# A fused SSM and token-mixing block: the short convolution of k for the fourth and fifth chunk, summed in place and moved out of step two

## The chip, the core and the metric

The kernel runs on one core of one Trainium2 chip. The metric is the device time of one execution in microseconds (us); the kernel's time is the median of its runs. TensorE (PE) multiplies matrices into PSUM, VectorE (DVE), ScalarE (ACT) and GpSimd (POOL) work on PSUM and SBUF (POOL on SBUF only, here), and SyncE (SP) issues the DMAs. Each engine takes its instructions in the order in which the program wrote them; they wait for one another by semaphores.

## The reference

```python
def _A_ref(q, k, v, shift_k, ssm_k, ssm_D):
    # short causal depthwise convolution of k (4 taps)
    k_pad = jnp.pad(k, ((0, 0), (ks - 1, 0), (0, 0)))
    for t in range(ks):
        k_shift = k_shift + k_pad[:, t:t + S, :] * shift_k[:, ks - 1 - t][None, None, :]
    kv = k_shift * v
    # long causal convolution of kv with ssm_k per channel, by FFT of length 2 S
    y = ... + kv * ssm_D
    return q * y

h = _layernorm(x) * (1 + ca) + sa
x = x + ga * _A_ref(h, A_k, A_v, A_shift_k, A_ssm_k, A_ssm_D)
h = _layernorm(x) * (1 + cb) + sb
x = x + gb * _B_ref(h, B_w1, B_b1, B_w2, B_b2)      # the token-mixing MLP with gelu
```

S = 2048 positions, D = 640 channels, F = 1728; sa to gb come from silu(c) @ w_mod. The change concerns `k_shift` and `kv` alone.

## The kernel before

The first part of the kernel, about 295 of its 669 us, does the long convolution in five chunks c = 0 to 4 of 128 channels (`NC = 5`). Each chunk's transform has stages on PE, and what the other engines do stands between them in the program's order, which is written out by hand (`manual_schedule`):

- *Step one* (`step1(side, t)`, line 230), four calls for the data (side 0, from tile `x`, which holds kv) and four for the kernel ssm_k (side 1, from `p`); ACT copies each result into `z`.
- *Step two* (`f2(g)`, line 249), eight groups g. PE multiplies `z` by constants into PSUM, ACT copies half of it into `kt`, then DVE forms two products per group (`p<-pst,kt`, called one group later) and POOL adds them into `y` (`y<-p`).
- *The inverses*: `i2(0)`, `i2(1)` (line 280) from `y` into `z`, then `i1(0)`, `i1(1)` (line 300). Among them stand step one of the next chunk: side 0, t = 0 and 1 ahead of `i2(0)`, t = 2 behind `i2(0)`, t = 3 behind `i2(1)`; side 1, t = 0 between `i1(0)` and `i1(1)`, t = 1 to 3 behind both. DVE scales q's part (`po`, `aux<-aux,g`) and multiplies the results by it, in `gate(c, ps, half)` (`aux<-pst,aux`); POOL adds that to x, SP writes x back (`spill`).

PSUM results of these stages take three buffers in turn (`psum()`, `ring = [0, 1, 2]`): the fourth result needs the buffer of the first.

The short convolution is DVE's side work. Tile `in` holds k's rows (`KX`: 3 rows of halo and 32 rows of 64 channels) and v's (`VX`). A chunk is done in four groups of eight rows. For a group, `kv_ops(g)` gives eight instructions of 128 x 512: one product into a sum in PSUM (`tap`), three pairs of a product into `kt` and an addition to the sum, and the product of the sum with v into `x`. After a group's product, `kv_loads` issues the loads of k and v for the next chunk into the rows that came free. `kv` strings the four groups together, and the list `fill` keeps what is not yet issued; `dv(n)` issues the next n of it at hand-chosen places. In an iteration c the convolution that is issued belongs to chunk c + 2.

For c = 1 and 2 (chunks 3 and 4), `dv(7)` stands ahead of `i2(0)`, `dv(3)` behind step one's t = 3, `dv(3)` between `i1(1)` and the second gate, `dv(11)` after the last step one: 24 of the 32 instructions. The eight that are left are issued in step two of iteration c + 1, between the products of its groups. The convolution of chunk 2 is put in `fill` in iteration 0 and runs mostly in step two of c = 1.

`load_ks(c + 2)` loads ssm_k for a later chunk; POOL adds ssm_D to it (`perm_add`) in step two of the next iteration.

Of the kernel before, what the change touches and what calls it, by code (L numbers as in the profile page):

```python
# [16 lines left out]
NC = D // DC  # L17
# [33 lines left out]
def mixer_kernel(ctx: ExitStack, tc: tile.TileContext, q, k, v, shift_k, ssm_k, ssm_D, w1, b1, w2, b2, c,  # L51
# [90 lines left out]
    def load_k(c, g, engs=(sync, sync)):  # L142
        for h in range(2):
            r = slice(64 * h, 64 * h + 64)
            engs[h].dma_start(KX[r, 3 + 8 * g:11 + 8 * g],
                           dram(k, 8 * g * D + DC * c + 64 * h, [[32 * D, 64], [D, 8], [1, 64]]))
# [7 lines left out]
    def load_halo(c):  # L154
        for h in range(2):
            sync.dma_start(KX[64 * h + 1:64 * h + 64, 0:3],
                           dram(k, 29 * D + DC * c + 64 * h, [[32 * D, 63], [D, 3], [1, 64]]))
# [27 lines left out]
    def kv_ops(g, eng=dve):  # L185
        S_, T_, W_ = (SV, TV, TAP) if eng is dve else (PS_.rearrange("p (n i) -> p n i", i=64),
                                                       PT.rearrange("p (n i) -> p n i", i=64), PW)
        w = lambda s: W_[:, None, s, :].to_broadcast([128, 8, 64])
        kx = lambda s: KX[:, 8 * g + 3 - s:8 * g + 11 - s, :]
        ops = [lambda: TT(eng, S_, kx(3), w(3), ALU.mult)]  # L190
        for s in (2, 1, 0):
            ops.append(lambda s=s: TT(eng, T_, kx(s), w(s), ALU.mult))
            ops.append(lambda: TT(eng, S_, S_, T_, ALU.add))
        ops.append(lambda: TT(eng, X.rearrange("p (n i) -> p n i", i=64)[:, 8 * g:8 * g + 8], S_,
                              VX[:, 8 * g:8 * g + 8], ALU.mult))
        return ops
# [11 lines left out]
    def kv(c_next, gs=((0,), (1,), (2,), (3,))):  # L208

        ops = []  # L210
        for gl in gs:
            o = kv_ops(gl[0])

            def end(gl=gl, last=o.pop()):
                last()
                if c_next is not None:
                    for g in gl:
                        kv_loads(c_next, g)
            ops += o + [end]
        return ops  # L220


    def step1(side, t, later=False):

# [313 lines left out]
    def dv(n):  # L538
        for _ in range(min(n, len(fill))):
            fill.pop(0)()  # L540

    x1s = lambda c, j: lambda: dve.bn_stats(bst[:, j, c, :], XR(j, DC * c, DC))
    for c in range(NC):
# [104 lines left out]
        elif cn is not None:  # L648
            for t in range(2):
                step1(0, t)  # L650
            perm(cn)
            if c + 2 < NC:
                fill.extend(kv(c + 3 if c + 3 < NC else None))
            else:
                fill.extend(x1s(cc, j) for cc in range(c) for j in range(16))
        else:
            t = mem("w1", 4096, "wb1")
            blk[1] = j16(t[:, 0:2048]), j16(t[:, 2048:4096])
            mod_load(3, 3, T_z[:, 0:1920])
            mod_load(3, 4, T_z[:, 1920:3840])  # L660
            sync.dma_start(P, wc[:, 2048:4096])
            for kk in range(3):
                mod_part(tap, kk, pl[kk])
            t = mem("in", 4288, "wb3")
            blk[3] = j16(t[:, 0:2048]), j16(t[:, 2048:4096])
            run(po)
            split_third(0, False, True)
            for f in (1, 3):
                split_third(f)
                split_rows(0, X, (f,))  # L670
                split_rows(1, T_aux[:, 0:2048], (f,))
            split_rows(0, X, (0,), False, True)
            split_rows(1, T_aux[:, 0:2048], (0,), False, True)
        if c:
            if cn is not None:
                dv(7)
            i2(0)
            if cn is None:
                split_rows(3, P, (1, 3))
                split_rows(3, P, (0,), True, False)  # L680
                mod_part(tap, 3, pl[3])
                i2(1, dve)
                mod_part(tap, 4, pl[4])
                t = mem("y", 4096, "wb2")
                blk[2] = j16(t[:, 0:2048]), j16(t[:, 2048:4096])
                break
            run(po)
            step1(0, 2)
            i2(1)
            step1(0, 3)  # L690
            dv(3 if cn < NC - 1 else 28)
        if c and c + 2 < NC:
            load_ks(c + 2)
        if cn == NC - 1:
# [7 lines left out]
        for half in range(2):  # L702
            ps = i1(half)
            if c and half:
                dv(3)
            elif c:
                k0 = step1(1, 0, True)
            gate(c, ps, half, pool if c else None)
# [412 lines left out]
    def product(n):  # L1121
        w_ = of(n)[1]
        bank[n] = psum()[:, 0:320]
        wh, wl = W.pop(n)
        for m, i in enumerate(SETS + ((6, 5) if n < 4 else (5, 6))):
            rh, rl = moving[w_](i)
            for k, (w, r) in enumerate(((wh, rh), (wh, rl), (wl, rh))):
                pe.matmul(bank[n], w[:, i].bitcast(F32R), r.bitcast(F32R), start=m == 0 and k == 0,  # L1128
                          stop=m == 6 and k == 2)
# [97 lines left out]
```

## Time and profile before

| | |
|---|---|
| median of 3 runs | 666.49 us (665.19 to 666.98) |
| profiled execution, its own time | 671.21 us |
| its span, first to last instruction | 669.4 us |
| PE busy | 619.5 us (93%) |
| DVE busy | 501.9 us (75%) |
| ACT busy | 309.7 us (46%) |
| POOL busy | 108.1 us (16%) |
| mean granted clock of PE | 0.982 |

Rows of the timeline give start, busy time, engine, line, operation, output<-input, and in brackets the idle time of the engine before it with what ended it. `SPq` is the time in which SP's queue issued a DMA. Rows of the table by windows give a stretch, its length, busy time of PE, PE's weight loads, DVE, ACT and POOL (with counts), the clock granted to PE, the share of the DMA engines' time and GB/s. Rows of the groups give how many instructions of a kind there are, their busy time and the mean of one in ns. Times are in us from the span's start.

### The profile page before, as it was taken

What the parts mean: (1) busy time and instruction counts of PE and PEld (TensorE: products, weight loads), DVE (VectorE), ACT (ScalarE), POOL (GpSimd) and SP (SyncE); (2) the same over time, 40 slices, a digit from 0 to 9 for tenths busy, and PEclk for the clock granted to TensorE, in tenths of its full rate; (3) what the DMA queues carried; (4) which work ended last, traced back from release to release, by engine and by line L of the source; (5) the groups of instructions that cost most, each with busy time, mean ns of one, the idle gap of its engine ahead of it and who ended that gap; (6) DMA issues with size and microseconds to landing.
All of it is one profiled execution on the core that took longest, in us unless ns stands there. A gap on an engine that the chain in (4) does not pass through costs nothing.

```text
span 669.4 us, 20749 instructions
## 1 busy us (share of the span) xinstructions
PE 619.5 (93%) x9073; PEld 597.8 (89%) x9073; DVE 501.9 (75%) x860; ACT 309.7 (46%) x483; POOL 108.1 (16%) x120
## 2 busy tenths in 40 slices
PE   0599878899998999999999999999999999999997
PEld 0598568788997989689999999999999999999997
DVE  6688569969969948789974213846689889888886
ACT  0574475545735647667765224334243332333331
POOL 5284027413324127000000000000000000000000
PEclk9999789999999999879999999999999999999999
DMA  9968988727438525414006630885598565345601
GB/s 179 213 194 225 391 172 159 168 54 165 83 70 221 180 51 156 172 33 95 0 1 126 119 71 1 189 234 144 174 365 268 173 179 154 102 144 169 188 31 41
DMA packets 175472, 98.01 MB, mean 146 GB/s; under 512 B 89843, under 2 KB 165398, under 8 KB 175126
## 3 DMA queue, kind: packets, MB, share of 16 engines
q1 hardware_dynamic: 170834, 95.38, 54.0%
q10 hardware_dynamic: 4548, 1.31, 1.1%
q8 instruction: 71, 1.16, 0.7%
q14 instruction: 19, 0.16, 0.1%
HBM read 79.63 MB, written 19.14 MB: 148 GB/s over the span
## 4 chain that ended last, share of the span: by engine, by line
PE 71%; DVE 16%; DMA 6%; issue 3%; SPq 2%; ACT 1%; POOL 0%; ACTq 0%; DVEq 0%; POOLq 0%
PE pst L1128 26%; PE pst L463 19%; PE pst L230 9%; PE pst L249 7%; PE pst L280 5%; PE pst L993 4%; DVE tap L60 3%; DVE kt L60 2%; DMA aux<-in_A_ssm_k_dram 2%; PE pst L300 2%; DMA aux<-in_w_mod_dram 2%; DVE p L60 1%; SPq L532 1%; PE tap L364 1%; DMA in<-in_A_k_dram 1%
## 5 line engine op out<-in xcount | busy, mean ns | idle before, releaser
L249 PE MATMUL pst<-z,w 128*64 128x64 f32 x2560 | 78.9, 223 | 11.0 <-DVE p L60 6.0
L249 PEld LDWEIGHTS pst<-z,w 128*64 128x64 f32 x2560 | 76.8, 138 | 13.7 <-issue 10.4
L230 PE MATMUL pst<-v,x 128*64 128x128 f32 x640 | 45.7, 302 | 24.2 <-DVE x L60 23.7
L230 PEld LDWEIGHTS pst<-v,x 128*64 128x64 f32 x640 | 43.6, 221 | 24.9 <-POOL t L488 23.7
L235 ACT ACTIVATE z<-pst 128x1024 f32<-128x1024 f32 (+2 forms) x45 | 41.4, 931 | 43.6 <-PE pst L230 24.9
L60 POOL TENSOR_TENSOR y<-p 128x256 f32<-128x256 f32 x72 | 54.1, 776 | 40.1 <-DVE p L60 39.7
L60 DVE TENSOR_TENSOR p<-pst,kt 128x512 f32<-128x512 f32 x80 | 50.8, 681 | 10.5 <-ACT kt L255 9.6
L280 PEld LDWEIGHTS pst<-v,y 32*128 32x128 f32 x1280 | 39.4, 193 | 4.2 <-issue 2.7
L280 PE MATMUL pst<-v,y 32*128 32x64 f32 x1280 | 41.2, 279 | 1.6 <-issue 1.0
L255 ACT ACTIVATE kt<-pst 128x512 f32<-128x512 f32 x40 | 23.9, 598 | 36.7 <-PE pst L249 20.9
L230 PE MATMUL pst<-v,p 128*64 128x128 f32 x640 | 37.3, 274 | 1.4 <-ACT p L177 1.2
L230 PEld LDWEIGHTS pst<-v,p 128*64 128x64 f32 x640 | 35.3, 137 | 2.2 <-ACT p L177 1.4
L1128 PE MATMUL pst<-r_z,m_w 128*128 128x320 f32 x198 | 37.2, 309 | 0.0
L60 DVE TENSOR_TENSOR tap<-tap,kt 128x512 f32<-128x512 f32 x51 | 35.5, 696 | 1.3
L60 DVE TENSOR_TENSOR kt<-in,tap 128x512 f32<-128x512 f32 x51 | 34.9, 685 | 1.5
L300 PEld LDWEIGHTS pst<-z,v 64*64 64x64 f32 x1280 | 24.7, 157 | 7.9 <-issue 3.5
L1128 PEld LDWEIGHTS pst<-r_z,m_w 128*128 128x128 f32 x198 | 31.1, 188 | 0.0
L300 PE MATMUL pst<-z,v 64*64 64x64 f32 x1280 | 26.9, 243 | 3.7 <-issue 2.4
L288 ACT ACTIVATE z<-pst 128x512 f32<-128x512 f32 x38 | 21.3, 664 | 18.3 <-PE pst L280 18.3
L1065 ACT ACTIVATE m_w<-m_v 128x896 fp32r<-128x896 f32 x19 | 17.9, 948 | 23.3 <-DVE m_v L60 13.0
L60 DVE TENSOR_TENSOR m_w<-m_v,m_w 128x896 fp32r<-128x896 f32 x19 | 20.6, 1086 | 6.5 <-ACT m_w L1065 6.5
L1128 PE MATMUL pst<-h_x,m_w 128*128 128x320 f32 x132 | 24.6, 309 | 0.0
(303 smaller groups left out, 1417.2 us busy)
## 6 DMA issues: line engine op xcount, KB each, us to landing
x<-in_B_w_dram SPq DMA_DIRECT2D x18, 512.0 KB
m_v<-in_B_w_dram SPq DMA_DIRECT2D x20, 384.0 KB
aux<-in_A_ssm_k_dram SPq DMA_DIRECT2D x10, 512.0 KB
out_dram<-m_w SPq DMA_DIRECT2D x32, 160.0 KB
in<-in_A_k_dram SPq DMA_DIRECT2D x36, 128.0 KB
in<-in_A_v_dram SPq DMA_DIRECT2D x36, 128.0 KB
ts<-m_p SPq DMA_DIRECT2D x10, 320.0 KB
m_w<-xs SPq DMA_DIRECT2D x20, 160.0 KB
```

The lines of the kernel that those rows point to most:

```text
L60: TT = lambda eng, o, a, b, op: eng.tensor_tensor(o, a, b, op=op)
L230: pe.matmul(ps.rearrange("p (b m a) -> p b a m", b=2, a=4)[64 * ri:64 * ri + 64, a // 4, a % 4], lhs, F1[:, 128 * ri:128 * ri + 128], star ...
L235: act.activation(Z[:, side, t, :, k0:k1], ps.rearrange("p (b k a) -> p b k a", b=4, a=4)[:, :, k0:k1], AF.Copy)
L249: pe.matmul(pk[64 * h:64 * h + 64, kk // 4, ri, kk % 4], W2[k1 // 32][:, 2 * (k1 % 32) + ri], rhs, start=True, stop=True)
L255: act.activation(halves_(kt), pv[:, :, 1], AF.Copy)
L280: pe.matmul(pp[qd // 2][:, o:o + 64], Y[p, ri, i:i + 2].rearrange("p i k -> p (i k)"), V2[p, 64 * ri:64 * ri + 64], start=ri == 0, stop=ri ...
L288: act.activation(o, i, AF.Copy)
L300: pe.matmul(ps[64 * b:64 * b + 64, 512 * e + 64 * jj:512 * e + 64 * jj + 64], V1[p, ri, n2], T2[p, :, 32 * ri + n2], start=ri == 0, stop=r ...
L463: pe.matmul(ps[0:m, h, 0:320], w_.bitcast(F32R), r_[:, 320 * h:320 * h + 320].bitcast(F32R), start=first and i == 0, stop=last and i == 2)
L993: pe.matmul(ps[n][:, h, 0:320], sets[n][:, j].bitcast(F32R), r[:, 320 * h:320 * h + 320].bitcast(F32R), start=j == 0 and r is hh, stop=j = ...
L1065: act.activation(W[n][0].bitcast(F32R), A[p, w_], AF.Copy)
L1128: pe.matmul(bank[n], w[:, i].bitcast(F32R), r.bitcast(F32R), start=m == 0 and k == 0, stop=m == 6 and k == 2)
```

## The change

For chunks 3 and 4 the list `kv` is replaced by `kv_late`. Groups are convolved from the last to the first (3, 2, 1, 0), and the last addition of each group writes the sum over k's own rows in `in`, so that the sum no longer has to be multiplied by v at once. Two products of 128 x 1024 then take two groups each: one behind groups 3 and 2, one behind 1 and 0; behind each, the next chunk's k and v for two groups are loaded (eight DMAs, and two for the halo behind the second). The list has 30 instructions instead of 32, and the counts of `dv` become 14, 4, 4 and 11, so that all 30 are issued in iteration c and none is left for step two.

```diff
--- before.py
+++ after.py
@@ -219,6 +219,23 @@
             ops += o + [end]
         return ops
 
+
+    def conv(g):
+        ops = kv_ops(g)[:6]
+        return ops + [lambda: TT(dve, KX[:, 3 + 8 * g:11 + 8 * g], SV, TV, ALU.add)]
+
+    def kv_late(c_next):
+
+        def product(g0, g1):
+            TT(dve, X.rearrange("p (n i) -> p n i", i=64)[:, 8 * g0:8 * g1], KX[:, 3 + 8 * g0:3 + 8 * g1],
+               VX[:, 8 * g0:8 * g1], ALU.mult)
+            if c_next is not None:
+                for g in range(g0, g1):
+                    load_k(c_next, g)
+                    load_v(c_next, g)
+                if g0 == 0:
+                    load_halo(c_next)
+        return conv(3) + conv(2) + [lambda: product(2, 4)] + conv(1) + conv(0) + [lambda: product(0, 2)]
 
     def step1(side, t, later=False):
 
@@ -650,7 +667,7 @@
                 step1(0, t)
             perm(cn)
             if c + 2 < NC:
-                fill.extend(kv(c + 3 if c + 3 < NC else None))
+                fill.extend(kv_late(c + 3 if c + 3 < NC else None))
             else:
                 fill.extend(x1s(cc, j) for cc in range(c) for j in range(16))
         else:
@@ -673,7 +690,7 @@
             split_rows(1, T_aux[:, 0:2048], (0,), False, True)
         if c:
             if cn is not None:
-                dv(7)
+                dv(14 if cn < NC - 1 else 7)
             i2(0)
             if cn is None:
                 split_rows(3, P, (1, 3))
@@ -688,7 +705,7 @@
             step1(0, 2)
             i2(1)
             step1(0, 3)
-            dv(3 if cn < NC - 1 else 28)
+            dv(4 if cn < NC - 1 else 28)
         if c and c + 2 < NC:
             load_ks(c + 2)
         if cn == NC - 1:
@@ -702,7 +719,7 @@
         for half in range(2):
             ps = i1(half)
             if c and half:
-                dv(3)
+                dv(4 if cn < NC - 1 else 3)
             elif c:
                 k0 = step1(1, 0, True)
             gate(c, ps, half, pool if c else None)
```

The order on DVE, with names of tiles as above (`DMAHW` are the counters by which DMAs report, `Activation`, `PE` and `DVE` the engines'). First, the start of the inverses in c = 1, behind the last additions of step two. Before:

```order
L60 TENSOR_TENSOR y<-p 128x2x16x4 [waits DVE_49] x2
L60 TENSOR_TENSOR y<-p 128x2x16x4 x2
L60 TENSOR_TENSOR tap<-in,tap 128x512 [waits DMAHW2_49,DMAHW1_49,DMAHW7_49,DMAHW0_49,Activation_49]
L60 TENSOR_TENSOR kt<-in,tap 128x512 [waits DVE_49]
L60 TENSOR_TENSOR tap<-tap,kt 128x512 [waits DVE_49]
```

And with the change:

```order
L60 TENSOR_TENSOR y<-p 128x2x16x4 [waits DVE_49] x2
L60 TENSOR_TENSOR y<-p 128x2x16x4 x2
L60 TENSOR_TENSOR tap<-in,tap 128x512 [waits DMAHW5_49,DMAHW2_49,DMAHW6_49,DMAHW1_49,Activation_49]
L60 TENSOR_TENSOR kt<-in,tap 128x512 [waits DVE_49]
L60 TENSOR_TENSOR tap<-tap,kt 128x512 [waits DVE_49]
```

The first product of the convolution stands at the same place, but reads group 3's rows of k and waits for the counters of the last two loads of k (groups 2 and 3) instead of those of group 0. Second, around the scaling `po` and the first gate of c = 1. Before:

```order
L60 TENSOR_TENSOR tap<-tap,kt 128x512 [waits DVE_49]
L60 TENSOR_TENSOR aux<-aux,g 128x2048
L60 TENSOR_TENSOR aux<-aux,g 128x2048 [waits DVE_49]
L60 TENSOR_TENSOR x<-tap,in 128x512 [waits DMAHW6_49,DMAHW5_49,PE_49]
L60 TENSOR_TENSOR tap<-in,tap 128x512 [waits DMAHW6_49,DMAHW5_49,DVE_49]
L60 TENSOR_TENSOR kt<-in,tap 128x512 [waits DVE_49]
L60 TENSOR_TENSOR aux<-pst_1900,aux 128x2x512 [waits PE_49]
```

And with the change:

```order
L60 TENSOR_TENSOR kt<-in,tap 128x512 [waits DVE_49]
L60 TENSOR_TENSOR in<-tap,kt 128x512 [waits DVE_49]
L60 TENSOR_TENSOR aux<-aux,g 128x2048
L60 TENSOR_TENSOR aux<-aux,g 128x2048 [waits DVE_49]
L60 TENSOR_TENSOR x<-in 128x1024 [waits DMAHW4_49,DMAHW3_49,DMAHW7_49,DMAHW0_49,PE_49]
L60 TENSOR_TENSOR tap<-in,tap 128x512
L60 TENSOR_TENSOR kt<-in,tap 128x512 [waits DVE_49]
L60 TENSOR_TENSOR tap<-tap,kt 128x512 [waits DVE_49]
L60 TENSOR_TENSOR aux<-pst_1914,aux 128x2x512 [waits PE_49]
```

`po` is the same two instructions, with seven more of the convolution ahead of them; between `po` and the gate stand the product of 1024 columns and three instructions of the convolution, where there were one product and two. Third, DVE from the end of c = 1 into step two of c = 2. Before:

```order
L60 TENSOR_TENSOR tap<-in,tap 128x512
L60 TENSOR_TENSOR kt<-in,tap 128x512
L60 TENSOR_TENSOR p<-pst_2135,kt 128x512 x2
L60 TENSOR_TENSOR tap<-tap,kt 128x512
L60 TENSOR_TENSOR kt<-in,tap 128x512
L60 TENSOR_TENSOR p<-pst_2173,kt 128x512 x2
L60 TENSOR_TENSOR tap<-tap,kt 128x512
L60 TENSOR_TENSOR p<-pst_2213,kt 128x512 x2
L60 TENSOR_TENSOR kt<-in,tap 128x512
L60 TENSOR_TENSOR p<-pst_2254,kt 128x512 x2
L60 TENSOR_TENSOR tap<-tap,kt 128x512
L60 TENSOR_TENSOR p<-pst_2297,kt 128x512 x2
```

And with the change:

```order
L60 TENSOR_TENSOR in<-tap,kt 128x512
L60 TENSOR_TENSOR x<-in 128x1024
L60 TENSOR_TENSOR p<-pst_2147,kt 128x512 x2
L60 TENSOR_TENSOR p<-pst_2183,kt 128x512 x2
L60 TENSOR_TENSOR p<-pst_2221,kt 128x512 x2
L60 TENSOR_TENSOR p<-pst_2261,kt 128x512 x2
L60 TENSOR_TENSOR p<-pst_2303,kt 128x512 x2
L60 TENSOR_TENSOR p<-pst_2343,kt 128x512 x2
```

The eight instructions that stood ahead of and between the groups' products are gone, and the last of the convolution is the product `x<-in` ahead of step two. PE, ACT and POOL keep their order. On SP, the loads of the next chunk's k and v stand in two blocks: eight behind the first product, ahead of the loads of ssm_D and ssm_k and of both spills, and ten behind the spills; before, two stood ahead and sixteen behind.

## The prediction

> **What bounds the kernel now.** I read the page's chain first, then TensorE's rows of the stages around the change, VectorE's rows there, and last the load queue. c counts the chunks from 0; "step two" is `f2`, eight groups of products; "the inverses" are `i2`, `i1` and the `step1` calls among them.
>
> ```profile
> PE 71%; DVE 16%; DMA 6%; issue 3%; SPq 2%; ACT 1%; POOL 0%; ACTq 0%; DVEq 0%; POOLq 0%
> ```
>
> TensorE (PE) carries the chain, so a change on VectorE (DVE) is worth what PE stops waiting for, less what PE begins to wait for. Step two of c=2 and of c=4, the latter without any convolution:
>
> ```profile
> 156.30:172.70 16.40, 15.57 (x511) 15.23 (x513) 16.16 (x27) 10.29 (x22) 8.95 (x14) 1.00 0.59 140
> 250.30:265.40 15.10, 15.10 (x515) 15.03 (x518) 11.56 (x18) 11.93 (x29) 10.43 (x12) 1.00 0.55 162
> ```
>
> The columns after the length are busy PE, PE's weight loads, DVE, ScalarE (ACT) and GpSimd (POOL). With convolution DVE is busy 16.16 of 16.40 us; without it, PE is busy throughout. PE's rows from the end of c=1 on:
>
> ```profile
> 143.13 2.10 PE L300 MATMUL pst<-z,v 64*64 64x64 f32 x128
> ...
> 150.40 5.46 PE L230 MATMUL pst<-v,p 128*64 128x128 f32 x96
> 156.30 5.82 PE L249 MATMUL pst<-z,w 128*64 128x64 f32 x192 [0.44 <-ACT z L235]
> 162.45 2.08 PE L249 MATMUL pst<-z,w 128*64 128x64 f32 x64 [0.34 <-DVE p L60]
> 164.98 7.90 PE L249 MATMUL pst<-z,w 128*64 128x64 f32 x255 [0.44 <-DVE p L60]
> ...
> 172.77 4.28 PE L230 MATMUL pst<-v,x 128*64 128x128 f32 x63
> ...
> 195.69 5.46 PE L230 MATMUL pst<-v,p 128*64 128x128 f32 x96
> 201.58 5.82 PE L249 MATMUL pst<-z,w 128*64 128x64 f32 x192 [0.43 <-ACT z L235]
> 207.72 2.08 PE L249 MATMUL pst<-z,w 128*64 128x64 f32 x64 [0.32 <-DVE p L60]
> 210.25 3.92 PE L249 MATMUL pst<-z,w 128*64 128x64 f32 x126 [0.44 <-DVE p L60]
> 215.92 4.40 PE L249 MATMUL pst<-z,w 128*64 128x64 f32 x130 [1.76 <-issue]
> 220.11 4.33 PE L230 MATMUL pst<-v,x 128*64 128x128 f32 x64
> 250.26 15.15 PE L249 MATMUL pst<-z,w 128*64 128x64 f32 x512 [0.44 <-ACT z L235]
> ```
>
> Step two takes 16.4 us in c=2 (156.30 to about 172.7) and 18.53 in c=3 (201.58 to 220.11), against 15.15 where DVE is free. Each time the fourth and fifth group wait for DVE's products. The 1.76 in c=3 is ended by no event of another engine.
>
> **What the change does to step two.** It takes eight VectorE instructions out of each of the two. ACT and POOL don't take over as the bound: in c=4 they do no less work per group (11.93 and 10.43 of 15.10 us) and PE runs through. So I price step two at c=4's length. c=2: 16.4 to 15.15, **-1.25**. c=3: the 1.76 I keep, since PE has the same instructions there: 18.53 to 16.91, **-1.62** (ends: -3.38 if it closes, 0.14 if another as long joins it).
>
> **What it does to the inverses of c=1.** The same convolution now stands at their front, fourteen instructions instead of seven, and the last rows come first. Before:
>
> ```profile
> 129.69 0.69 DVE L60 TENSOR_TENSOR tap<-in,tap 128x512 f32<-128x512 f32 x1
> ...
> 134.04 0.70 DVE L60 TENSOR_TENSOR tap<-tap,kt 128x512 f32<-128x512 f32 x1
> 134.65 4.61 DVE L60 TENSOR_TENSOR aux<-aux,g 128x2048 f32<-128x2048 f32 x2
> 143.21 0.69 DVE L60 TENSOR_TENSOR x<-tap,in 128x512 f32<-128x512 f32 x1 [3.96 <-PE pst L230]
> ...
> 145.30 1.22 DVE L60 TENSOR_TENSOR aux<-pst,aux 128x1024 f32<-128x1024 f32 x1
> ...
> 150.51 1.28 DVE L60 TENSOR_TENSOR aux<-pst,aux 128x1024 f32<-128x1024 f32 x1 [1.92 <-PE pst L300]
> ...
> 161.03 1.28 DVE L60 TENSOR_TENSOR p<-pst,kt 128x512 f32<-128x512 f32 x2
> ...
> 175.73 0.69 DVE L60 TENSOR_TENSOR tap<-in,tap 128x512 f32<-128x512 f32 x1
> ```
>
> Seven convolution instructions take 5.05 us (129.69 to 134.74), 0.721 each; the scaling `po` (aux<-aux,g) 4.52; a gate (aux<-pst,aux) about 1.2. DVE sat idle 3.96 us before 143.21, which is the room the seven extra ones move into. New is the product over 1024 columns, x<-in, two operands from SBUF. The nearest row:
>
> ```profile
> L60 DVE TENSOR_TENSOR wb0b<-x,wb0b 128x1024 fp32r<-128x1024 f32 x8 | 9.4, 1221 | 5.8 <-ACT wb0b L452 5.5
> ```
>
> The lower end is half of one `po` instruction, 1.15; the upper is two of today's products, 1.38. I take 1.25. That the sum's last addition now writes SBUF instead of PSUM I cost at nothing: x<-tap,in at 143.21 writes SBUF too and takes 0.69, tap<-tap,kt 0.70. Per chunk DVE's work shrinks by 4 x 0.69 - 2 x 1.25 = 0.26 us, on no path.
>
> DVE's new order is 14 convolutions (10.1), `po` (4.52), product (1.25), 3 convolutions (2.17), gate 0 (1.2), 4 convolutions (2.89), gate 1 (1.2). From 129.69 gate 0 would end at 148.9 and gate 1 at 153.0. PE waits for both. Its buffers go round in threes, so the `step1` that starts at 150.40 needs the one gate 0 empties, and the third of the three (150.40 + 2 x 1.82 = 154.04) that of gate 1; PE follows DVE by 0.14 (161.03 + 1.28 to 162.45). That leaves spare 1.4 us at gate 0 and 0.9 at gate 1: without a stall the front costs nothing.
>
> But a stall there will be. Group 3's rows of k are the last that the queue loads for this chunk, and DVE now begins with them:
>
> ```profile
> 129.33 2.40 SPq L145 DMA_DIRECT2D in<-in_A_k_dram  x2
> 131.82 1.22 SPq L161 DMA_DIRECT2D rows<-in_A_shift_k_dram  x2
> ```
>
> ```profile
> 131.00:131.80 0.80, 0.80 (x33) 0.80 (x32) 0.77 (x2) 0.75 (x1) 0.00 (x0) 1.00 0.08 14
> 131.80:132.60 0.80, 0.80 (x40) 0.80 (x35) 0.73 (x3) 0.80 (x2) 0.00 (x0) 1.00 0.72 165
> 132.60:133.40 0.80, 0.80 (x40) 0.80 (x33) 0.77 (x2) 0.80 (x1) 0.00 (x0) 1.00 0.73 172
> 133.40:134.20 0.80, 0.80 (x37) 0.80 (x36) 0.77 (x2) 0.66 (x1) 0.00 (x0) 1.00 0.50 121
> 134.20:135.00 0.80, 0.80 (x24) 0.73 (x22) 0.80 (x2) 0.22 (x1) 0.00 (x0) 1.00 0.24 51
> ```
>
> The second half of that load leaves the queue at 131.73. Last column, GB/s: almost nothing moves up to 131.8, then 132 + 138 + 97 + 41 = 408 KB, which is these 256 KB of k and the 128 KB of taps behind them. So k's bytes are in at about 133.4, the earliest end. A row for issue to use:
>
> ```profile
> 88.99 5.13 SPq L145 DMA_DIRECT2D in<-in_A_k_dram  x4
> ...
> 96.88 2.52 POOL L60 TENSOR_TENSOR t<-in,t 128x512 f32<-128x512 f32 x2 [1.63 <-DMA in<-in_A_k_dram]
> ```
>
> Issued by 94.12, used at 96.88, 2.76 later, with a fuller link; here that gives 134.5. The latest end is 135.0, when the traffic stops. I take 134.0: DVE waits 4.3 us. Behind its first instruction stand `po` and both gates, behind those PE and POOL's additions to x. Gate 1's spare of 0.9 comes off: **+3.4 us** (2.8 to 4.4).
>
> After gate 1 (157.3) come 7 convolutions and a product, 6.3 us, instead of eleven and more: step two's first products end at about 164.9, and PE needs them for its fourth group at 165.4. No wait.
>
> **The inverses of c=2.** Its k and v were loaded long before. The same sums from 175.73: gate 0 ends at 194.9, PE needs it at 195.69; gate 1 at 199.0, PE needs it at 199.33. With the 0.14, 0.2 us remain: **0**, at worst +0.5.
>
> **Queues.** The 18 loads of c=1 for the last chunk stay 18, but SP now issues eight behind the first product instead of two, ahead of the ssm_k load and both spills:
>
> ```profile
> 146.17 3.91 SPq L167 DMA_DIRECT2D aux<-in_A_ssm_k_dram  x2
> 165.69 0.77 POOL L60 TENSOR_TENSOR aux<-aux,rows 1x64 f32<-1x64 f32 x2
> ```
>
> Product ending near 149.9, eight issues at 0.65 and a pause like the one above, the small load, then 3.91: ssm_k is issued by 161, 11 us later than today. POOL's use of it would fall near 167.5, and it may slip by some 2 us more before a later group of step two feels it. I cost it at nothing; this cover is thin, and is in the third rival.
>
> **Sum:** +3.4 - 1.25 - 1.62 = +0.5 us on the profiled execution (span 669.4, its own time 671.21). It lies 4.7 above the median of the runs, 666.49; these stages run at full clock, so I carry the difference over: **667.0 us**. The ends of the terms make 664.7 (2.8 - 1.25 - 3.38) to 669.3 (4.4 - 1.25 - 1.62, and the next paragraph's 1.3).
>
> **A row and a rule on TensorE's clock.** PE would sit idle from 150.5 to 153.3, longer than anywhere in the trace once it has started. Rows of granted clock (the figure before the DMA share):
>
> ```profile
> 86.90:90.32 3.42, 1.85 (x39) 1.24 (x43) 0.50 (x1) 3.42 (x9) 0.00 (x0) 0.98 0.45 60
> 90.32:93.73 3.41, 3.39 (x126) 3.20 (x120) 3.34 (x4) 3.13 (x9) 0.35 (x1) 0.52 1.10 192
> 213.19:216.60 3.41, 1.65 (x54) 1.51 (x51) 2.88 (x5) 0.91 (x3) 2.87 (x5) 1.00 0.87 266
> 216.60:220.01 3.41, 3.33 (x116) 3.25 (x111) 2.38 (x4) 2.40 (x6) 1.74 (x3) 1.00 0.87 284
> ```
>
> After 1.57 idle of 3.42 the clock fell to 0.52 for 3.4 us; after 1.76 idle of 3.41 it stayed at 1.00. So 2.8 us idle may cost a slow stretch. Its price: 126 matmuls where full clock does 207 in the same 3.41 us (128 of that kind at 143.13 took 2.10), 1.3 us. The Trainium skill, "TensorE: Matmul & The Clock Gate", in the section on the HAM clock gate, has the clock halve only after a whole idle window of about 3.4 us; by it the sum stays at +0.5. The rows at 86.90 and 90.32 don't agree with that, those at 213.19 do.
>
> **The rivals.**
> - Faster: k's last rows are in when DVE asks. For it: the link is idle up to 131.8. Against: their second half leaves the queue only at 131.73. With no stall -2.9 remains, **663.6**; it is faster by over 2.0 us from a landing before about 131.5 on, which leaves a loss of 0.9.
> - Slower by the clock: the slow stretch above, +0.5 + 1.3 = +1.8, **668.3**; half of such outcomes pass +2.0.
> - Slower, step two not shortened: ssm_k late at POOL, or GpSimd's additions in the way, hold its later groups as long as DVE does today. c=4's row speaks against it. Then +3.4, **669.9**.
> - The change not doing what it says: the instruction order shows no convolution left in these two step twos, so no chance is kept for that.
>
> **How the numbers follow.** 0.3% is 2.0 us, about what a measurement of this kernel tells from no change. Forecast 0.50, within 2.0 us either way. Faster rival 0.19. Clock 0.20, of it 0.14 beyond +2.0. Step two not shortened 0.11. That makes faster 0.19, same 0.50 + 0.06 = 0.56, slower 0.14 + 0.11 = 0.25. The range 664.3 to 669.6 takes in the forecast's ends and the clock, and leaves out most of the faster rival and the worst of the last: 2 in 10.
>
> **What would show it.** Right: DVE idle some 4.3 us at about 129.7, ended by the load of k; PE's `step1` near 150.4 delayed by 2.9 us for a gate and its third by 3.4; step two at about 15.2 us in c=2 and 15 to 17 in c=3, with no wait for p; after c=2's gates no wait of PE. Wrong: no idle time ended by k; a granted clock under 1.00 near 154; a wait of POOL for ssm_k; new gaps of PE without a releaser.

## The result, and the profile after

The changed kernel takes 675.72 us (median of 4 runs, 674.38 to 676.56) against 666.74 us of the kernel before on the same chip (665.19 to 668.19): ratio 1.011, interval 1.008 to 1.014. It is slower by 9.0 us; I had forecast 667.0 us, in a range up to 669.6. The profiled execution has a span of 674.5 us and took 676.45 us itself.

Lines have moved by 17: step one is L247, step two L266, `i2` L297, `i1` L317. PE's rows of the timeline from the end of c=1's inverses to step two of c=4 (start, busy time, engine, line, operation, in brackets the idle time before and what ended it):

```profile
147.73 0.62 PE L317 MATMUL pst<-z,v 64*64 64x64 f32 x25 [0.24 <-issue]
154.46 7.40 PE L247 MATMUL pst<-v,p 128*64 128x128 f32 x96 [6.11 <-DVE aux L60]
162.30 15.36 PE L266 MATMUL pst<-z,w 128*64 128x64 f32 x511 [0.44 <-ACT z L252]
...
177.56 4.39 PE L247 MATMUL pst<-v,x 128*64 128x128 f32 x63
...
196.76 1.97 PE L247 MATMUL pst<-v,p 128*64 128x128 f32 x32 [0.52 <-PE pst L317]
...
207.01 11.43 PE L266 MATMUL pst<-z,w 128*64 128x64 f32 x382 [0.43 <-ACT z L252]
220.38 3.98 PE L266 MATMUL pst<-z,w 128*64 128x64 f32 x127 [1.94 <-issue]
226.63 0.41 PE L266 MATMUL pst<-z,w 128*64 128x64 f32 x3 [2.27 <-issue]
226.76 5.62 PE L247 MATMUL pst<-v,x 128*64 128x128 f32 x64
...
258.06 15.50 PE L266 MATMUL pst<-z,w 128*64 128x64 f32 x512 [0.44 <-ACT z L252]
```

Three things are new. PE stands 6.11 us for the first gate of c=1, the 96 products of step one behind it take 7.40 us instead of 5.46, and step two of c=3 has two gaps that no other engine ends (1.94 and 2.27) instead of one of 1.76. The two waits of step two for `p` are gone, and c=2's step two takes 15.2 us (162.30 to 177.5) instead of 16.4. VectorE's rows of the same place, in the same form:

```profile
135.42 0.70 DVE L60 TENSOR_TENSOR tap<-in,tap 128x512 f32<-128x512 f32 x1 [6.91 <-DMA in<-in_A_k_dram]
...
145.47 4.61 DVE L60 TENSOR_TENSOR aux<-aux,g 128x2048 f32<-128x2048 f32 x2
150.00 1.22 DVE L60 TENSOR_TENSOR x<-in 128x1024 f32<-128x1024 f32 x1
```

The first product of the convolution waits 6.91 us for k's rows; fourteen instructions and `po` run behind it without a pause, and gate 0 ends at 154.40, 0.06 before PE starts. SP's queue issued those rows here:

```profile
130.86 1.31 SPq L145 DMA_DIRECT2D in<-in_A_k_dram  x2
```

It was done at 132.17, and VectorE started 3.25 us later. The clock, in the table by windows (length, busy PE, weight loads, DVE, ACT, POOL, then the granted clock, the share of the DMA engines and GB/s):

```profile
147.50:151.00 3.50, 0.62 (x25) 0.48 (x25) 3.46 (x3) 1.02 (x1) 0.00 (x0) 1.00 0.03 5
151.00:154.50 3.50, 0.04 (x2) 0.05 (x2) 3.43 (x6) 0.00 (x0) 0.00 (x0) 0.59 0.39 89
154.50:158.00 3.50, 3.50 (x34) 3.50 (x36) 3.40 (x5) 0.00 (x0) 2.36 (x1) 0.50 0.85 192
158.00:161.50 3.50, 3.50 (x64) 3.50 (x62) 3.36 (x6) 2.06 (x2) 2.38 (x1) 0.93 0.96 159
```

PE is granted half its clock from about 151.7 on, while it idles, and for some 4 us after it has started again. From c=1's first step one to step two of c=4 the changed kernel takes 132.59 us (125.47 to 258.06), the kernel before 123.54 (126.72 to 250.26): 9.05 more. The medians differ by 9.0; that the two agree so well is partly luck, as the second pair of profiles will show.

### The profile page after: what moved, and what is told of

It is laid out like the page before. It is cut to its first block, busy times and chain, and to the rows that moved or that the text cites. A ratio compares the mean times of both kernels' runs of the same rounds, so it can differ in the third digit from the quotient of the medians.

```text
span 674.5 us, 20730 instructions
## 1 busy us (share of the span) xinstructions
PE 617.1 (91%) x9073; PEld 596.9 (88%) x9073; DVE 502.0 (74%) x856; ACT 309.6 (46%) x483; POOL 107.7 (16%) x120
## 3 DMA queue, kind: packets, MB, share of 16 engines
q8 instruction: 71, 1.16, 0.7%
## 4 chain that ended last, share of the span: by engine, by line
PE 74%; DVE 17%; DMA 3%; issue 3%; ACT 2%; SPq 0%; ACTq 0%; DVEq 0%
PE pst L1145 26%; PE pst L480 19%; PE pst L247 10%; PE pst L266 9%; PE pst L297 4%; PE pst L1010 3%; DVE tap L60 3%; DVE kt L60 2%; DVE aux L60 2%; PE pst L317 2%; DMA v<-in_const_v_dram 1%; PE tap L381 1%; DVE p L60 1%; DMA in<-in_A_k_dram 1%; DVE xb L799 1%
## 5 line engine op out<-in xcount | busy, mean ns | idle before, releaser
L266 PE MATMUL pst<-z,w 128*64 128x64 f32 x2560 | 78.4, 223 | 11.6 <-issue 5.0
L266 PEld LDWEIGHTS pst<-z,w 128*64 128x64 f32 x2560 | 76.5, 138 | 14.0 <-issue 10.5
L247 PE MATMUL pst<-v,x 128*64 128x128 f32 x640 | 47.2, 308 | 24.0 <-DVE x L60 23.5
L247 PEld LDWEIGHTS pst<-v,x 128*64 128x64 f32 x640 | 45.1, 221 | 24.7 <-POOL t L505 23.5
L247 PE MATMUL pst<-v,p 128*64 128x128 f32 x640 | 38.8, 283 | 6.9 <-DVE aux L60 6.1
L247 PEld LDWEIGHTS pst<-v,p 128*64 128x64 f32 x640 | 37.1, 143 | 7.5 <-DVE aux L60 6.2
L297 PEld LDWEIGHTS pst<-v,y 32*128 32x128 f32 x1280 | 38.5, 190 | 4.3 <-issue 2.9
L297 PE MATMUL pst<-v,y 32*128 32x64 f32 x1280 | 40.2, 275 | 1.8 <-issue 1.2
L60 DVE TENSOR_TENSOR tap<-tap,kt 128x512 f32<-128x512 f32 x43 | 30.0, 698 | 1.3
L317 PEld LDWEIGHTS pst<-z,v 64*64 64x64 f32 x1280 | 22.4, 144 | 7.5 <-issue 3.7
L317 PE MATMUL pst<-z,v 64*64 64x64 f32 x1280 | 24.4, 230 | 4.3 <-issue 2.6
L914 ACT ACTIVATE pst<-pst,sm 128x640 f32<-128x640 f32 x14 | 10.7, 765 | 31.1 <-PE pst L480 31.1
```

Source lines behind the costliest of these rows:

```text
L60: TT = lambda eng, o, a, b, op: eng.tensor_tensor(o, a, b, op=op)
L247: pe.matmul(ps.rearrange("p (b m a) -> p b a m", b=2, a=4)[64 * ri:64 * ri + 64, a // 4, a % 4], lhs, F1[:, 128 * ri:128 * ri + 128], star ...
L266: pe.matmul(pk[64 * h:64 * h + 64, kk // 4, ri, kk % 4], W2[k1 // 32][:, 2 * (k1 % 32) + ri], rhs, start=True, stop=True)
L297: pe.matmul(pp[qd // 2][:, o:o + 64], Y[p, ri, i:i + 2].rearrange("p i k -> p (i k)"), V2[p, 64 * ri:64 * ri + 64], start=ri == 0, stop=ri ...
L317: pe.matmul(ps[64 * b:64 * b + 64, 512 * e + 64 * jj:512 * e + 64 * jj + 64], V1[p, ri, n2], T2[p, :, 32 * ri + n2], start=ri == 0, stop=r ...
```

## The experiments

Twelve further runs were made, in four groups; each group has its own runs of the kernel before. For all but x_fill and x_idle I read the starts of step two (the row that ACT's `z` ends, as at 162.30 above) of c = 1, 2, 3 and 4 from their profile. The three parts between them hold everything that the change touches:

| kernel | starts (us) | c=1 | c=2 | c=3 | sum | ratio to before |
|---|---|---|---|---|---|---|
| before | 105.39 156.30 201.58 250.26 | 50.9 | 45.3 | 48.7 | 144.9 | 1 |
| before, second profile | 106.74 157.14 203.27 251.17 | 50.4 | 46.1 | 47.9 | 144.4 | 1 |
| changed | 104.45 162.30 207.01 258.06 | 57.9 | 44.7 | 51.1 | 153.6 | 1.011 (1.008 to 1.014) |
| changed, again (x_after) | 103.77 157.92 202.50 253.35 | 54.2 | 44.6 | 50.9 | 149.6 | 1.013 (1.009 to 1.017) |
| in c=1 alone (x_c1) | 103.18 161.24 205.75 255.70 | 58.1 | 44.5 | 50.0 | 152.5 | 1.005 (1.002 to 1.008) |
| in c=2 alone (x_c2) | 105.96 155.27 201.07 251.90 | 49.3 | 45.8 | 50.8 | 145.9 | 1.001 (0.998 to 1.004) |
| k's last rows first (x_order) | 106.74 156.11 202.00 253.32 | 49.4 | 45.9 | 51.3 | 146.6 | 1.000 (0.996 to 1.004) |
| the same again (x_order2) | 102.62 153.53 199.34 249.20 | 50.9 | 45.8 | 49.9 | 146.6 | 1.001 (0.997 to 1.005) |
| order reversed only (x_rev) | 111.78 162.18 207.72 256.06 | 50.4 | 45.5 | 48.3 | 144.3 | 0.999 (0.995 to 1.003) |
| w_mod behind the spill (x_mod) | 104.48 160.03 204.77 251.88 | 55.6 | 44.7 | 47.1 | 147.4 | 1.015 (1.011 to 1.019) |
| order, and w_mod later (x_both) | 106.23 155.81 202.06 256.90 | 49.6 | 46.3 | 54.8 | 150.7 | 1.010 (1.006 to 1.014) |
| c=1 alone, with order (x_one) | 104.37 157.07 201.94 249.75 | 52.7 | 44.9 | 47.8 | 145.4 | 1.003 (1.000 to 1.007) |

**x_order: k's last rows loaded first.** The change stays whole; only the loads that feed c=1's convolution come in another order.

```diff
-            fill.extend(kv(3, ((0,), (1, 2), (3,))))
+            fill.extend(kv_first())    # groups 0, 3, 1 and 2; loads of k: rows 3, 2, then 0, 1
```

> The changed kernel with chunk 2's groups taken in the order 0, 3, 1 (2 stays on GpSimd) and the loads for chunk 3 put behind them so that k's rows of groups 3 and 2 are loaded first and those of groups 0 and 1 last. Theory S (k's last rows come late and the fourteen instructions carry that to the gates): VectorE starts its convolution in c = 1 without idle time, TensorE's wait of 6.1 us for the first gate and the slow clock behind it go, 667 to 669 us. Rival D (fourteen instructions ahead of the scaling make the gates late by themselves): TensorE still waits for the gates in c = 1, 673 to 676 us. Rival F (what is lost is lost in step two of c = 3, in TensorE's gaps without a releaser): 674 to 676 us.

VectorE no longer waits for k in c=1, the first part falls to 49.4 us, and nothing of the loss is left in the median: ratio 1.000. TensorE waits for no gate in c=1, so rival D falls; rival F falls as the cause of the loss, though the third part is as long as in the changed kernel. A second time, on another chip:

> The changed kernel with only c=0's order of groups altered (0, 3, 1 and 2, so that the queue loads k's last rows first), a second time, since the changed kernel itself was timed beside other runs of the kernel before. If the stall on k's last rows, with the slow clock behind it, makes the main loss, the ratio is again 0.996 to 1.005, against 1.011 and 1.013 of the unaltered change; the first part (from step two of c=1 to that of c=2) takes 49 to 50.5 us with no wait for k, and c=3's step two keeps its two gaps (third part about 51 us). If the first time was chance, the ratio is 1.008 to 1.015.

1.001. PE's rows of this second profile at the place of the stall:

```profile
147.08 0.62 PE L332 MATMUL pst<-z,v 64*64 64x64 f32 x25 [0.43 <-issue]
...
153.53 11.66 PE L281 MATMUL pst<-z,w 128*64 128x64 f32 x388 [0.44 <-ACT z L267]
```

No wait for a gate stands between them. So the loss of the median hangs on the order in which k's rows are loaded; but a gain over the kernel before isn't there either. The third part is still longer than before.

**x_c1 and x_c2: the change in one chunk only.** `kv_late` and its counts in c=1 alone, and in c=2 alone.

```diff
-                fill.extend(kv_late(c + 3 if c + 3 < NC else None))
+                fill.extend((kv_late if c == 1 else kv)(c + 3 if c + 3 < NC else None))    # x_c2: c == 2
-                dv(14 if cn < NC - 1 else 7)
+                dv(14 if c == 1 else 7)    # the counts of 4 likewise
```

> Only the fourth chunk is convolved in the new way, in c = 1; the fifth as before in c = 2 and in step two of c = 3. S: the idle time of 6 to 7 us in c = 1, TensorE's wait of about 6 us and the slow clock stay, step two of c = 2 is 1.25 us shorter: 671 to 674 us. D: half of the change's loss, 670 to 672 us. F: nothing lost, 665 to 667 us.

> Only the fourth chunk's list stays as before (counts 7, 3, 3, 11 in c = 1); the fifth chunk is convolved in the new way in c = 2. S: in c = 2 k's last rows have left the queue 2.3 us before VectorE asks, so the idle time is at most 1 us and TensorE loses at most 0.8; the 16.4 us of step two in c = 2 stay; 666 to 669 us. D: the gates of c = 2 come late by 3 us or more, 669 to 672 us. F: as the change in c = 3, two gaps of about 2 us, 668 to 671 us.

VectorE's and PE's rows of x_c1, then the end of c=3's step two in x_c2:

```profile
133.61 0.70 DVE L60 TENSOR_TENSOR tap<-in,tap 128x512 f32<-128x512 f32 x1 [6.15 <-DMA in<-in_A_k_dram]
152.65 8.15 PE L247 MATMUL pst<-v,p 128*64 128x128 f32 x96 [5.29 <-DVE aux L60]
```

```profile
215.16 3.98 PE L266 MATMUL pst<-z,w 128*64 128x64 f32 x127 [2.22 <-issue]
221.42 0.33 PE L266 MATMUL pst<-z,w 128*64 128x64 f32 x3 [2.27 <-issue]
```

The stall and the slow 96 products come with c=1's half of the change; x_c2 has no stall in its first part, and in c=2 its PE waits only 0.64 and 0.19 us for the gates (at 194.76 and 198.66), within what theory S had. The time of x_c1 is another matter: 1.005 is some 3.4 us, less than the 4.5 to 7.5 of theory S, while its profile loses 7.2 us in the first part alone (58.1 against 50.9). A longer third part comes with c=2's half (50.8 us). It isn't its alone: x_c1 has 50.0 with gaps of 2.03 and 1.18, x_one and the kernel before, which lack that half too, have 47.8 to 48.7. The two ratios, 1.005 and 1.001, add up to less than the 1.011 of the whole; their intervals reach to 1.008 and 1.004, so this gap isn't resolved.

**x_rev: the order of groups alone.** The kernel before with its groups 3, 2, 1, 0 and everything else, the counts of `dv` too, as it was.

```diff
-                fill.extend(kv(c + 3 if c + 3 < NC else None))
+                fill.extend(kv_rev(c + 3 if c + 3 < NC else None))    # for g in (3, 2, 1, 0)
```

> The kernel before with the four groups of chunks 3 and 4 taken from the last to the first, not in place, with the old counts (7, 3, 3, 11) and each group's loads behind its product: the wait for k's last rows without the seven extra instructions. S: VectorE sits idle some 6 us at the start of the inverses of c = 1, ended by the load of k, but seven instructions fewer stand ahead of the gates, which come within 0.5 us of TensorE's need: 666 to 669 us. Rival (a stall there costs its length, whatever follows it): 672 to 674 us.

No loss, 0.999. VectorE's two waits ahead of the first gate of c=1:

```profile
137.08 0.70 DVE L60 TENSOR_TENSOR tap<-in,tap 128x512 f32<-128x512 f32 x1 [0.81 <-DMA in<-in_A_k_dram]
...
149.62 0.69 DVE L60 TENSOR_TENSOR x<-tap,in 128x512 f32<-128x512 f32 x1 [2.97 <-PE pst L245]
```

Its first product waits for k's last rows as well, but 0.81 us and not the 6 expected, and only seven instructions stand ahead of `po`, so that 2.97 us of idle time ahead of its next product remain as room. In this profile step two of c=1 began 6.4 us later than in the kernel before (111.78 against 105.39), so it says little on the length of the wait. The order alone cost nothing; but behind a wait as short as this one neither theory would show a loss that the medians can tell. That a stall of 6 us costs because seven more instructions have taken up the room behind it is argued from VectorE's rows, not shown by this run.

**x_after: the changed kernel again.**

> The changed kernel again, unaltered, to have its ratio beside the other kernels of this group and a second profile. Theory S (VectorE's first convolution of c=1's inverses stands about 7 us for k's last rows, TensorE then idles about 6 us at the gate, and its clock falls behind that idle): the wait of 6 us before the 96 step1 products of c=1 and their slow length of 7.4 to 8.2 us (5.46 at full clock) come again; ratio 1.007 to 1.013. Theory R (the 9 us between the two medians are mostly the spread of the runs, and the stall is worth no more than the +3.4 of the prediction): the wait is nearer to 3 us, ratio 1.000 to 1.005.

The loss repeats (1.013), but this profile has a shorter stall:

```profile
131.33 0.69 DVE L60 TENSOR_TENSOR tap<-in,tap 128x512 f32<-128x512 f32 x1 [2.84 <-DMA in<-in_A_k_dram]
150.36 7.13 PE L247 MATMUL pst<-v,p 128*64 128x128 f32 x96 [1.66 <-DVE aux L60]
```

The expectation of 6 us fell, and that of theory R for the ratio too. Over five profiles of kernels with `kv_late` in c=1 and the old order of loads, VectorE waited 2.84, 3.67 (x_fill), 6.15, 6.51 (x_mod) and 6.91 us. The queue's last issue of k ended at 128.35 in this one, and VectorE was ready at 128.49; in the first it was 132.17 against 128.51. What varies is mostly the queue, whose pairs of issues take 1.27 us or, at changing places, 1.4 to 2.5 us.

**x_idle: what an idle time alone does to the clock.** The kernel before, with VectorE held up by products into scratch.

```diff
+            if not half:
+                for _ in range((0, 8, 11, 0, 0)[c]):
+                    TT(dve, TV, KX[:, 27:35, :], TAP[:, None, 0, :].to_broadcast([128, 8, 64]), ALU.mult)
             gate(c, ps, half, pool if c else None)
```

> The kernel before, with VectorE kept busy in front of the first gate of the inverses: 8 extra products of 512 columns in c=1 and 11 in c=2 (into scratch, used by nobody); no load is moved. VectorE has 3.9 us to spare there, and 8 x 0.72 = 5.8 and 11 x 0.72 = 7.9 us are added, so TensorE should idle about 1.9 us at c=1's gate and 4.0 us at c=2's. If an idle time alone sets the clock back and 1.7 us are enough for it (as in the second profile of the changed kernel), both are followed by a granted clock of 0.50 for 4 to 6 us and 96 step1 products of 7 us instead of 5.46. If a whole idle window of 3.4 us is needed, only the second is. If the loads of the changed kernel do it, neither is.

```profile
150.68 7.13 PE L230 MATMUL pst<-v,p 128*64 128x128 f32 x96 [2.25 <-DVE aux L60]
...
202.59 7.12 PE L230 MATMUL pst<-v,p 128*64 128x128 f32 x96 [4.52 <-DVE aux L60]
```

And the clock behind the first of them, by windows:

```profile
147.50:151.00 3.50, 0.94 (x31) 0.80 (x33) 3.43 (x5) 1.02 (x1) 0.23 (x1) 1.00 1.01 159
151.00:154.50 3.50, 3.50 (x42) 3.50 (x38) 3.40 (x6) 0.70 (x1) 2.68 (x2) 0.56 0.47 73
```

Both idle times, 2.25 and 4.52 us, are followed by the slow clock, and 96 products take 1.67 us longer than at full clock, with no load moved. So a late gate is enough for the slow stretch, without the loads of the changed kernel. It is one profile, without a time to compare.

**x_fill: an attempt to keep PE busy in the stall.**

```diff
+            if c == 1 and half:
+                for i in range(96):
+                    pe.matmul(tap[0:64, 768:896], KSP[:, i % 32], F1[:, 0:128], start=True, stop=True)
```

> The changed kernel with 96 extra products on TensorE behind i1's second half in c=1 (into a corner of PSUM that nobody reads), which are to keep it busy while VectorE is late: about 5.4 us of work in an idle time of about 6.1. They compute nothing that is used. If the clock falls because TensorE stands idle, the granted clock stays at 1.00 through 160, the 96 step1 products take 5.5 us instead of 7.4, and the part from c=1's first step1 to step two of c=2 is about 1.9 us shorter than in the changed kernel (34.9 instead of 36.8); the ratio falls by 0.003 against the changed kernel. If the clock falls for another reason, such as the traffic of the loads that begins then, nothing moves: 36.8, and 0.5 in the rows at 152 to 158.

It took 1.042 (1.038 to 1.046) and answers nothing on the clock. The extra products, 192 in the trace, wrote into the tile in which VectorE keeps its sum, and VectorE waited for them as they for it:

```profile
148.43 21.07 PE L723 MATMUL tap<-v,p 128*64 128x128 f32 x191 [1.39 <-DVE tap L60]
169.65 0.69 DVE L60 TENSOR_TENSOR kt<-in,tap 128x512 f32<-128x512 f32 x1 [20.14 <-PE tap L723]
```

The clock stayed at 1.00 there, but PE had idled 1.39 us only.

**x_mod and x_both: the loads of w_mod in c=3 moved.** In x_mod they are issued behind the spill; x_both has the order of x_order, and the loads one place later.

```diff
-            for kk in range(2):
-                mod_load(3, kk, ...)
-            for j in range(3):
-                sync.dma_start(pl[2][j], dram(w_mod, ...))
             load_rows(1, T_aux[:, 0:2048])
+            ...    # x_both: the five loads here; x_mod: behind spill(c)
```

> The changed kernel with c=3's first loads of w_mod (two of 1920 columns, three pieces of 640) issued after the spill, behind step two of c=3, instead of at its middle; everything else as it is. Theory L (the second unattributed gap of TensorE in c=3's step two, 2.27 us, comes because VectorE frees k's place 5 us earlier there, so that these loads run while TensorE's own instructions are fetched): the second gap goes or falls under 0.7 us, the first of 1.94 may stay; step two of c=3 17 us instead of 19.7; ratio 0.003 below the changed kernel's. Theory K (the gaps come from the place in TensorE's instruction stream): both stay, 1.9 and 2.3 us.

> The changed kernel with two repairs: in c=0 the groups go 0, 3, 1 and 2 so that the queue loads k's last rows for c=1 first (as in the kernel with that alone), and in c=3 the five loads of w_mod are issued behind the load of the next rows instead of ahead of it. If the stall of c=1 and the second gap of c=3's step two are the whole loss, then from the start of c=1's step two on the three parts to the starts of step two of c=2, c=3 and c=4 take about 49.4, 45.2 and 48.5 us or less (143, against 144.4 to 144.9 before), and the ratio is 0.996 to 1.000: two terms of about -1.2 us remain of the change. If the loads only meet TensorE's instructions at another place, a gap of 1 to 2.5 us without a releaser stands elsewhere in c=3 or in c=4's step two, and the ratio is 1.000 to 1.003.

x_mod, PE from c=3's step two into c=4's, and the issue of its loads:

```profile
217.86 4.40 PE L266 MATMUL pst<-z,w 128*64 128x64 f32 x130 [1.67 <-issue]
...
260.75 3.95 PE L266 MATMUL pst<-z,w 128*64 128x64 f32 x127 [1.37 <-issue]
...
266.50 3.94 PE L266 MATMUL pst<-z,w 128*64 128x64 f32 x127 [1.80 <-issue]
```

```profile
252.31 1.65 SPq L374 DMA_DIRECT2D in<-in_w_mod_dram  x2
```

The second gap of c=3 is gone (third part 47.1 us) while the first stays with 1.67, and two gaps of 1.37 and 1.80 have come up in c=4's step two, which had none; the ratio is no better. In x_both the loads are issued from 230.21 on, and long gaps now stand in c=3's inverses:

```profile
216.25 5.31 PE L281 MATMUL pst<-z,w 128*64 128x64 f32 x130 [2.77 <-issue]
...
239.23 0.62 PE L262 MATMUL pst<-v,x 128*64 128x128 f32 x6 [1.75 <-issue]
...
245.25 0.34 PE L332 MATMUL pst<-z,v 64*64 64x64 f32 x6 [3.39 <-issue]
```

Whether the second gap opens is thus set by these loads, as theory L had it; its forecast of a lower ratio fell. The places themselves are old ones: the 3.39 stands ahead of the last 6 of 128 products of `i1`, where the kernel before has 0.92 (at 239.90). The longest gap outlasts the traffic. The stretch ahead of the 3.39, by windows:

```profile
241.00:243.00 2.00, 0.86 (x54) 0.72 (x46) 0.00 (x0) 0.00 (x0) 0.00 (x0) 1.00 0.92 344
243.00:245.30 2.30, 0.05 (x3) 0.05 (x3) 0.00 (x0) 0.00 (x0) 0.00 (x0) 1.00 0.04 14
```

PE stops under a full link and starts again some 2 us after the link has fallen still. x_both is slower than the kernel before (1.010) though it has no stall, so it matters where the loads are moved to.

**x_one: the change in c=1 alone, with the order of x_order.** The edits of x_c1 and x_order together.

> The change in c=1 alone, with the same order of groups in c=0, so that no stall on k's last rows is left; c=2 and with it c=3's step two stay as before. Expected parts 49.4, 44.7 to 45.5 and 48.3 us (142.4 to 143.2): 1.2 to 2.4 us under before, ratio 0.996 to 0.999, too little to be told from no change. If the loads of c=0 that are now issued in another order cost something in their turn, the first part is over 50.4 us and the ratio over 1.000.

1.003: not faster. The third part is as before (47.8), the second shows the gain (44.9), but the first took 52.7 us in this profile. In c=1 PE stood four times 1.2 to 1.6 us for VectorE's products in step two, which x_order2 has as well (50.9), and 1.52 us without a releaser in the inverses, where x_order2 has 0.43. No version that ran is shown to beat the kernel before.

**x_before: the kernel before again.**

> The kernel before, unaltered, for a second profile. If the gaps of TensorE in c=3's step two and the slow clock at 86 to 94 us belong to the kernel, they come again: one gap of about 1.8 us, and the part from c=1's first step1 to step two of c=4 takes 123.5 us within 0.5. If they vary from run to run, that part varies by 1 to 2 us, and single terms of under 1.5 us can't be read from one profile of each kernel.

```profile
217.09 4.12 PE L249 MATMUL pst<-z,w 128*64 128x64 f32 x130 [1.21 <-issue]
```

One gap, 1.21 instead of 1.76. The sum of the parts agrees within 0.5 us, single parts differ by up to 0.9. Terms of about one microsecond are not to be read from one pair of profiles.

## Why the prediction was wrong, step by step

**The stall: mechanism right, size wrong.** I had VectorE wait 4.3 us; it was 6.91. VectorE came 1.18 us earlier (128.51 against 129.69), the queue was done 0.44 later (132.17 against 131.73), and the rows were usable 3.25 us after that instead of my 2.27; together 2.60. The room that I took off, 0.9, was gate 1's, and gate 1 cost nothing: PE runs the 96 products behind gate 0, at half its clock, without a wait (154.46, 7.40). At gate 0, where I had 1.4 of room, 6.91 of waiting became 6.11 of idle time on PE. Counted from c=1's first step one, PE started these products 5.31 us later than in the kernel before (154.46 less 125.47 against 150.40 less 126.72); that is the size of the term that I had at 3.4. The step that failed is that I took both ends of the wait from one profile as if they were fixed to one another. The profiles show 2.84 to 6.91 for VectorE's wait with the same order of loads; my ends of 3.7 and 5.3 for the wait (2.8 to 4.4 for the loss) came from readings of the landing alone.

**The clock: a rival at 0.20 that came.** In each of the seven waits of PE for a late gate of 1.66 us or more that the profiles show (1.66, 1.87, 2.25, 4.52, 5.29, 5.98 and 6.11; the 1.87 in c=0 of x_rev, at 104.60, with 1.37 more idle just ahead of it), the clock was halved behind it, and the 96 products took 6.80 to 8.15 us instead of 5.46. I had priced it at 1.3; it was 1.94 in the first profile. I had made it a rival of the stall though it is its consequence, and the stall itself was the forecast: its price belonged into the sum. An idle time of 1.52 us in x_one left the clock at 1.00, and so did gaps that no engine ended of 1.82 (x_c2, at 99.04) and 2.77 us (x_fill, at 233.12), so the length alone doesn't decide it. The Trainium skill, "TensorE: Matmul & The Clock Gate", in the section on the HAM clock gate, has the clock halve after a whole idle window of about 3.4 us. The idle times of 1.66 and 2.25 don't agree with that, those of 1.82 and 2.77 do.

**Step two of c=2: right.** -1.25 was forecast; 15.2 us came instead of 16.4, with no wait for `p`. The new product took 1.22 us (forecast 1.25). The inverses of c=2 lost 0.6 (forecast 0, at worst 0.5), the most of it 0.52 us in which step one waits for a buffer; the second profile of the kernel before has 0.61 at the same place, so I don't charge it to the change.

**Step two of c=3: wrong in sign.** I kept its gap of 1.76 "since PE has the same instructions there" and took off 1.62. Instead it lost time: 19.7 us instead of 18.53, two gaps, and a slow clock behind them (5.62 us instead of 4.33 for 64 products at 226.76). The failed step is the reason given: PE's instructions fix where a gap can stand, but not how long it is or whether a second one opens. In all 13 profiles without extra products on PE, a gap stands behind 382 of this stage's 512 products (192 + 64 + 126 in the kernel before), with 0.39 (x_rev) to 2.77 us (x_both); where there is a later one, it stands behind 509. What changed is the traffic. With VectorE out of c=3's step two, the tile `in` is free earlier, and the loads of w_mod into it go out 8.4 us behind the start of step two (215.45 less 207.01) instead of 10.9 (212.51 less 201.58); in the kernel before, their issue also takes 3.98 us instead of 1.08. Windows of c=3's step two in the changed kernel:

```profile
219.00:221.00 2.00, 0.62 (x19) 0.62 (x20) 0.00 (x0) 0.26 (x1) 0.57 (x1) 1.00 1.03 390
...
223.00:225.00 2.00, 1.36 (x47) 1.28 (x43) 1.29 (x2) 1.04 (x3) 1.48 (x3) 1.00 1.03 396
225.00:227.00 2.00, 0.36 (x5) 0.36 (x6) 0.00 (x0) 0.00 (x0) 0.55 (x1) 0.94 0.67 252
```

PE stops while the DMA engines are full, near 400 GB/s. That these loads decide on the second gap is shown by x_mod and x_both; the first stands in x_mod without them. That PE waits for its own instructions in such a gap is argued, from the list of DMA queues:

```profile
q8 instruction: 71, 1.16, 0.7%
```

71 packets brought instructions; 9073 products by 71 are 128 to a packet, and the gaps lie 127 products apart (x127 at 220.38). The Trainium skill, "Runtime: NRT & Kernel Launch", under Terms, says that an engine's instruction memory is refilled in blocks of 16 KiB; the trace agrees, with 1.16 MB in 71 packets, 16.3 KB each. The profile of x_fill bears it out. Its 192 extra products stand earlier in PE's program, and in c=3's step two its gaps lie behind 191, 318 and 445 products instead of 255, 382 and 509 (x_c2 has all three, the one behind 255 with 0.16 us): 64 earlier, as blocks of 128 would have it (192 less 128), and the queue brought 72 packets instead of 71.

```profile
220.30 5.81 PE L266 MATMUL pst<-z,w 128*64 128x64 f32 x191 [0.44 <-ACT z L252]
226.31 4.04 PE L266 MATMUL pst<-z,w 128*64 128x64 f32 x127 [0.19 <-issue]
233.12 3.98 PE L266 MATMUL pst<-z,w 128*64 128x64 f32 x127 [2.77 <-issue]
239.37 2.21 PE L266 MATMUL pst<-z,w 128*64 128x64 f32 x67 [2.27 <-issue]
```

So the gaps go with the blocks of PE's instructions. No run took the instructions' path away, so that PE stands for a late block stays the likeliest reading and not a shown one.

**The queue.** ssm_k was issued by 160.82, as forecast (161), and POOL did not wait for it. The rival in which step two isn't shortened did not come.

**From the profile to the median.** I carried the difference of two profiled executions over to the medians. The executions differ by 5.2 us (676.45 less 671.21), the medians by 9.0. From step two of c=4 on, where nothing was changed, the first profiles take 416.4 us with the change (674.5 less 258.06) and 419.1 before (669.4 less 250.26), and the other kernels that alter nothing there take 416 to 421: a spread half as large as the effect. The kernel's own profiled run lay 4.5 us above its median of 666.74, the changed one's 0.7 above. Carrying over was a step without a basis. The difference in the touched stages alone, 9.05, came nearer in this pair of profiles, but not in the second pair.

**The account.** Forecast +3.4, -1.25, -1.62 and 0; in the first pair of profiles c=1 cost 7.25 (125.47 to 162.30, 36.83, against 126.72 to 156.30, 29.58), c=2 gave 0.57 (44.71 against 45.28), and c=3 cost 2.37 (51.05 against 48.68): 9.05. The 7.25 is 5.31 for the late gate and 1.94 for the clock. The same sums from the second pair, x_after against x_before, give +2.92 for c=1 (157.92 less 125.44 against 157.14 less 127.58), -1.55 and +2.95: 4.32, for a ratio of 1.013, some 8 us. So the term of c=3 was wrong in both pairs (-1.62 against +2.37 and +2.95); that of c=1 was too small in the first only, and held +3.4 against 2.92 in the second because the clock's 1.67, which I had left out, made up for a shorter stall. What the rest of the median's loss consists of, where the stall is short, stays open.

## What to carry to other kernels

Before work is moved ahead of a gate, ask which load brings its operands and where that load stands in its queue: the order of fourteen instructions was harmless, their first operand was not. The length of such a wait is a difference between a queue and an engine that drift by microseconds from run to run, and a PE that waited some 2 us or more for a gate was slow for another 3 to 6 behind it; both belong to the price of the forecast itself. And when an engine lets go of a tile earlier, find the load that was waiting for the tile, and look at what else the DMA engines carry at the time when it will now run.

## What the hardware showed that I had not expected

- The granted clock fell to 0.50 behind waits of PE of 1.66 and 2.25 us for a gate, and stayed at 1.00 behind gaps of 1.52, 1.82 and 2.77 that no engine ended; the stretch of 0.50 lasted about 3.5 to 7 us. Behind the gaps of c=3's step two it fell in some profiles (1.94 and 2.27 in the changed kernel) and not in others (2.22 and 2.27 in x_c2).
- The last rows of k, two loads of 128 KB, were usable 2.27 us (x_fill) to 3.88 us (x_c1) after the queue had issued them, with 2.98 and 3.25 in the two profiles of the changed kernel.
- Gaps of PE without a releaser stand at fixed places of PE's instructions, 127 products apart in c=3's step two; which of them open, and for how long, follows transfers that have nothing to do with PE's operands. Moving five loads closed one of 2.27 us in c=3's step two and opened others of 1.4 to 3.4 us in later stages.
